# Block-sparse attention into a squared-ReLU feed-forward: an earlier load, more paired score slots, some inverses on VectorE, four more slots masked on TensorE

## Chip, cores, metric

One core of one Trainium2 chip. The metric is the device time in microseconds (us), median of several executions; lower is better. Engines: PE is TensorE (PEld its weight loads), DVE is VectorE, ACT is ScalarE, POOL is GpSimd, SP issues most DMAs.

## Reference

Four batches of eight heads, 768 positions, head size 64. The mask is made of 32 x 32 blocks: neighbours, the first and last block row and column, and three drawn blocks per block row. The attention output, 3072 x 512, goes through a feed-forward layer.

```
scores = (q @ k.T) / 8 ;  scores = where(mask, scores, -1e9)
attn   = softmax(scores) ;  x = attn @ v           # (4, 8, 768, 64) -> (3072, 512)
y      = (relu(x @ w_in) ** 2) @ w_out             # 512 -> 2048 -> 512
```

## The kernel before

Heads are handled in 16 pairs (four per batch). The unit of attention is a slot: one pair of heads, 256 queries (`qi`, three per sequence) and 256 keys (`cp`, three per sequence). There are 144 slots, 36 per batch. A slot has four score matmuls on 64 rows each (two heads side by side in the array: the two matmuls start some 4 ns apart in the trace), one exp on ACT, a multiplication by the mask on DVE, and four value matmuls on 128 rows. Three slots of one `qi` end in an inverse of the row sums (two Ln and an Exp on ACT) and two normalizing multiplications on DVE, which free `po`.

In batch 0 some slots are masked on PE instead: four more 64-row matmuls add a large negative number to the scores, and DVE has nothing to do.

```
def scores(slots):                        # one slot, or a pair of slots in a row
    for u, qi, cp in slots:
        ps = ps_s.tile([P, 2, 2, QW], F32, tag="ps")          # two such buffers in PSUM
        add = u < HP and qi < NQ_ADD
        for c in range(2 if add else 0):
            for h, hs in enumerate(HALVES):
                matmul(ps[:, h, c, :], oh[hs, ksl[c]], bq[hs, qsl], start=c == 0, stop=False)
        for c in range(2):
            for h, hs in enumerate(HALVES):                   # 64 rows per head
                matmul(ps[:, h, c, :], KT[i][hs, ksl[c]], QT[i][hs, qsl], start=not add, stop=True)

def inverse(u, qi):
    nc.scalar.activation(out=ls[0:D, :], in_=po[D:P, 0, :], func=AF.Ln)
    nc.scalar.activation(out=ls[D:P, :], in_=po[0:D, 1, :], func=AF.Ln)
    nc.scalar.activation(out=rs, in_=ls, func=AF.Exp, scale=-1.0)
```

The order of instructions on each engine is made when the kernel is built: every piece of work is a task with an engine, an estimated duration, a priority and its dependencies, and a list scheduler in the kernel's source places them. Attention has priority; feed-forward work of earlier batches fills PE.

```
# numbers of buffers, as handed to the scheduler:
bufs = {"ps": 2, "po": 1, "h": 2, "y": 1, "pT": 9, "r": 4, ...}
PAIRED = lambda s: s >= 72               # from slot 72 on (batch 2), two slots are one task
ld_t = Task("SP", 1.3, ..., (lambda u=u: load(u)), deps=... + gate[-1:], late=2.0, dma=3.9, ...)
# gate: a DMA that waits for the last piece of w_in (for pair 4), then of w_out (for pair 5 on)
```

The softmax here doesn't subtract the row's maximum and nothing guards it: scores larger than these inputs give would overflow.

Of the kernel before, what the change touches and what calls it, by code (L numbers as in the profile page):

```python
# [16 lines left out]
AF = mybir.ActivationFunctionType  # L17
AOP = mybir.AluOpType

P = 128  # L20
# [5 lines left out]
def kernel(  # L26
# [18 lines left out]
    nc = tc.nc  # L45
    B, H, S, D = q.shape
# [5 lines left out]
    scale = 1.0 / math.sqrt(D)  # L52
    assert D == 64 and S % P == 0 and d_model == moe_w_in.shape[0] and H % 2 == 0
    NCH = S // P
    HP = H // 2
    NF = d_ff // P
    KM = d_model // P
    QW = 256
    NQ = S // QW
    CP = NCH // 2  # L60
# [135 lines left out]
    V, G = nc.vector, nc.gpsimd  # L196
# [8 lines left out]
    def init_v(eng, i):  # L205
        eng.memset(VA[i][:, :, D:P], 1.0)
        eng.memset(VB[i][:, :, 0:D], 1.0)
# [70 lines left out]
    bq = consts.tile([P, S], BF, name="bq")  # L278
    mask = consts.tile([P, NQ, NCH, QW], BF, name="mask")
    mtile = {}  # L280
# [3 lines left out]
        nc.tensor.matmul(pb, bm.rearrange("a t j -> a (t j)"), oh[0:nb, qi * QW:(qi + 1) * QW], start=True, stop=True)  # L284
        mtile[qi] = pb

    def rows_copy(qi):
        nc.scalar.copy(out=bq[:, qi * QW:(qi + 1) * QW], in_=mtile.pop(qi))

    def mask_product(qi, cp):  # L290
        pq = ps_h.tile([P, 2, QW], F32, name="pq", tag="h")
# [50 lines left out]
    def w_load(i):  # L342

        if i < NWP:
            fs = slice(i * d_ff // NWP, (i + 1) * d_ff // NWP)
            nc.gpsimd.dma_start(out=w_in_sb[:, :, fs], in_=wiv[:, :, fs])
        else:
            ns = slice((i - NWP) * NF // NWP, (i - NWP + 1) * NF // NWP)
            nc.gpsimd.dma_start(out=w_out_sb[:, ns, :], in_=wov[:, ns, :])
# [4 lines left out]
        nc.sync.dma_start(out=scratch, in_=last)  # L354


    ptile, stile, otile, rtile, xT = {}, {}, {}, {}, {}

    def scores(slots):
        for u, qi, cp in slots:  # L360
            i = u % NPB
            ps = ps_s.tile([P, 2, 2, QW], F32, name="ps", tag="ps")
            qsl = slice(qi * QW, (qi + 1) * QW)
            ksl = [slice((cp * 2 + c) * P, (cp * 2 + c + 1) * P) for c in range(2)]
            add = u < HP and qi < NQ_ADD
            for c in range(2 if add else 0):
                for h, hs in enumerate(HALVES):
                    nc.tensor.matmul(ps[:, h, c, :], oh[hs, ksl[c]], bq[hs, qsl], start=c == 0, stop=False,  # L368
                                     skip_group_check=True)
            for c in range(2):  # L370
                for h, hs in enumerate(HALVES):
                    nc.tensor.matmul(ps[:, h, c, :], KT[i][hs, ksl[c]], QT[i][hs, qsl], start=not add,  # L372
                                     stop=True, skip_group_check=True)
            stile[u, qi, cp] = ps
# [28 lines left out]
            nc.tensor.matmul(po[:, 1, :], VB[i][:, n, :], pT[:, 1, c, :],  # L403
                             start=False, stop=last, skip_group_check=True)

    def inverse(u, qi):
        po = otile[u, qi]
        ls = work.tile([P, QW], F32, name="ls", tag="ls")
        rs = work.tile([P, QW], F32, name="rs", tag="rs")
        nc.scalar.activation(out=ls[0:D, :], in_=po[D:P, 0, :], func=AF.Ln)  # L410
        nc.scalar.activation(out=ls[D:P, :], in_=po[0:D, 1, :], func=AF.Ln)  # L411
        nc.scalar.activation(out=rs, in_=ls, func=AF.Exp, scale=-1.0)  # L412
        rtile[u, qi] = rs

    def normalize(u, qi):
# [78 lines left out]
            load_part(nc.sync, u, 0, c, c + 1)  # L494

    NQ_ADD = 2
    NQ_Y = 1
    KR, KY = 0, 500
    COLD = 5.3
    PT_BUFS, R_BUFS, G_BUFS, QC_BUFS = 9, 4, 2 * NF + 3, 5  # L500
# [6 lines left out]
    SEM = dict(late=LAT)  # L507
    pe = dict(late=0.2)
    order = [(a, qi, cp) for qi in range(NQ) for a in range(HP) for cp in range(CP)]
# [3 lines left out]
    first = {}  # L513
    for s, (u, qi, cp) in enumerate(order):
        first.setdefault(u, s)
    ev, cv, sc_of, va_of, mu = {}, {}, {}, {}, {}
    for u in range(NU):
        sc_of[u], va_of[u] = [], []
    wl, tr, gate, mk, tp = {}, {}, [], {}, {HP - 1: []}
# [9 lines left out]
    rc = []  # L529
    for qi in range(NQ):  # L530
        rp = Task("PE", 0.107, -7 if qi == 0 else 6 * qi - 6, (lambda qi=qi: rows_product(qi)), get="h",
                  deps=[oh_t] if qi else [], after=4.0 if qi == 0 else 7.0 * qi, **pe)
        rc.append(Task("ACT", 0.37, -7 if qi == 0 else 6 * qi - 6, (lambda qi=qi: rows_copy(qi)), deps=[rp], put=[rp], **SEM))
    for qi in range(NQ):
        for cp in range(CP):
            k = (qi - NQ_ADD) % NQ * CP + cp
# [5 lines left out]
    def prepare_first(u):  # L542

        tr[u], ev[u] = [], {}
        parts = [(1, c0, c1, t, first[u]) for (c0, c1), t in zip(K_PARTS.get(u, [(0, CP)]), land_k[u])]
        parts += [(0, c, c + 1, land_q[u][c], c * HP * CP + first[u]) for c in range(CP)]
        for w, c0, c1, at, s in parts:
            n = c1 - c0
            a = (u, w, c0, c1)
            on = "POOL" if c0 and not w else "ACT" if u == 0 and not c0 else "DVE"  # L550
            c = Task(on, 0.06 + {"DVE": 0.17, "POOL": 0.36, "ACT": 0.31}[on] * n, s - 6,
                     (lambda a=a, e={"DVE": V, "POOL": G, "ACT": nc.scalar}[on]: cast_qk(e, *a)), get="qc", after=at, **SEM)
            t = Task("PE", 0.15 * n, s - 5 - w, (lambda a=a: transp(*a)), deps=[c], get="h", put=[c], **pe)
            e = Task("DVE", 0.06 + 0.17 * n, s - 5, (lambda a=a: evac(*a)), deps=[t], put=[t], **SEM)
            tr[u].append(c)
            for i in range(c0, c1):
                ev[u][w, i] = e
        cv[u] = [Task("POOL", 0.6, first[u] - 2, (lambda u=u, h=h: cast_v(u, h)), after=land_v[u], **SEM)
                 for h in range(2)]
        if u == HP - 2:  # L560

            for i in range(NWP):
                wl[i] = Task("POOL", 1.0, first[u] + i, (lambda i=i: w_load(i)), deps=cv[u], late=2.0,
                             dma=3.4)
            gate.append(Task("SP", 0.5, 0, (lambda: loads_gate(1)), deps=[wl[NWP - 1]], late=0.0))

    def prepare(u):
        s0 = first[u]

        ld_t = Task("SP", 1.3, s0 - 20, (lambda u=u: load(u)), deps=cv[u - NRAW] + tr[u - NRAW] + gate[-1:],  # L570
                    late=2.0, dma=3.9, behind=tp[u - 1] if u > HP + 1 else [])
        old_sc = sc_of[u - NPB] if u >= NPB else []
        old_va = va_of[u - NPB] if u >= NPB else []
        tr[u], ev[u], tp[u] = [], {}, []
        for w in (1, 0):
            c = Task("DVE" if w else "POOL", 0.6 if w else 1.2, s0 - 12,
                     (lambda w=w: cast_qk(V if w else G, u, w, 0, CP)), deps=[ld_t], get="qc", **SEM)
            t = Task("SP", 1.5, s0 - 12, (lambda w=w: transp_dma(u, w)), deps=[c] + old_sc, put=[c],
                     late=2.0, dma=1.5)
            tr[u].append(c)  # L580
            tp[u].append(t)
            for i in range(CP):
                ev[u][w, i] = t
        early = []
        if u < NPB:
            early = [Task("POOL", 0.8, s0 - 8, (lambda u=u: init_v(G, u)), after=36.0, **SEM)]
        cv[u] = [Task("POOL", 0.6, s0 - 12, (lambda u=u, h=h: cast_v(u, h)), deps=[ld_t] + old_va + early, **SEM)
                 for h in range(2)]
        if u == HP:
            for i in range(NWP, 2 * NWP):  # L590
                wl[i] = Task("POOL", 1.0, s0 - 12 + i, (lambda i=i: w_load(i)), deps=cv[u], late=2.0, dma=4.0)
            gate.append(Task("SP", 0.5, 0, (lambda: loads_gate(2)), deps=[wl[2 * NWP - 1]], late=0.0))

    N_FIRST = HP * NQ_ADD * CP
    PAIRED = lambda s: s >= 72

    def attend(s, slots):
        sc = Task("PE", 0.645 if len(slots) > 1 else 0.56 if s < N_FIRST else 0.42, s, (lambda: scores(slots)),
                  deps=[t for u, qi, cp in slots if qi < NQ_ADD and u < HP for t in (rc[qi], oh_t)[:1 + (cp > 0)]] + [ev[u][1, cp] for u, qi, cp in slots] + [ev[u][0, qi] for u, qi, cp in slots] + sc_all[-1:],
                  get="ps", n=len(slots), **pe)  # L600
        sc_all.append(sc)
        for j, a in enumerate(slots):
            u, qi, cp = a
            k = s + j
            ex = Task("ACT", 0.97, k, (lambda a=a: exps(*a)), deps=[sc], get="pT", put=[sc.bufs[j]], **SEM)
            mm = ex
            if u >= HP or qi >= NQ_ADD:
                mm = Task("DVE", 0.82, k - 1, (lambda a=a: mask_mul(V, *a)), deps=[ex, mk[qi, cp]], **SEM)
            va = Task("PE", 0.44, k + 2.2, (lambda a=a: values(*a)), deps=[mm] + cv[u] + va_all[-1:],
                      get=None if cp else o_pool(u, qi), put=[ex], **pe)  # L610
            va_all.append(va)
            sc_of[u].append(sc)
            va_of[u].append(va)
            if cp == CP - 1:
                inv = Task("ACT", 1.2, k - 9, (lambda u=u, qi=qi: inverse(u, qi)), deps=[va], **SEM)
                mu[u, qi] = Task("DVE", 0.87, k - 9, (lambda u=u, qi=qi: normalize(u, qi)), deps=[inv],
                                 put=[va_all[-CP]], **SEM)

# [85 lines left out]
```

## Time and profile before

| | kernel before |
|---|---|
| median time | 313.33 us (312.79 to 314.36, 3 runs) |
| span of the profiled run | 311.1 us |
| PE busy | 297.7 us, 96% |
| ACT, DVE busy | 223.5 us, 214.0 us |
| last exp ends | 263.6 us; feed-forward work alone after it |

The span is the time between the first and last instruction of the program; the time has some 1.7 us more.

### The profile page before, as it was taken

The numbers are of one execution on the slowest core, as the hardware profiler recorded it, in microseconds if no ns is written. First come the engines' busy times: TensorE is split into PE (matmuls) and PEld (weight loads), VectorE is DVE, ScalarE is ACT, GpSimd is POOL, SyncE is SP. The second block draws the span as 40 slices with busy tenths as digits, with TensorE's granted clock in tenths as the row PEclk, the third lists the DMA queues.
The fourth block names the chain that finished last, engine by engine and source line by source line (L and its number), as shares of the span: only waits on it lengthen the run. The fifth ranks groups of instructions, "written<-read, shape, count | busy, mean of one in ns | idle before, by whom it ended". The sixth has DMA issues, their size and how long they took to land.

```text
span 311.1 us, 6029 instructions
## 1 busy us (share of the span) xinstructions
PE 297.7 (96%) x2259; PEld 173.3 (56%) x2292; DVE 214.0 (69%) x383; ACT 223.5 (72%) x358; POOL 178.4 (57%) x226
## 2 busy tenths in 40 slices
PE   6989889999999999999999999999999999999995
PEld 4655556557656545556555565555555655555542
DVE  8625559996967968998976668887657666444521
ACT  3899799985877989878878988888778887200000
POOL 5660396445974936975764457664454354666620
PEclk9999999999999999999999999999999999999999
DMA  7998289417447474716620083450000010000012
GB/s 221 346 208 169 90 140 184 152 37 201 105 147 223 94 200 151 215 48 211 163 75 36 1 238 87 151 86 27 9 34 36 0 37 35 34 36 34 34 36 101
DMA packets 42597, 34.47 MB, mean 111 GB/s; under 512 B 20680, under 2 KB 39624, under 8 KB 42568
## 3 DMA queue, kind: packets, MB, share of 16 engines
q1 hardware_dynamic: 37656, 29.50, 32.7%
q0 software_dynamic: 4224, 4.19, 8.4%
q10 hardware_dynamic: 688, 0.39, 0.4%
q8 instruction: 18, 0.29, 0.4%
q14 instruction: 11, 0.09, 0.1%
HBM read 27.26 MB, written 6.29 MB: 108 GB/s over the span
## 4 chain that ended last, share of the span: by engine, by line
PE 79%; DVE 9%; ACT 7%; issue 3%; POOL 1%; DVEq 0%; ACTq 0%
PE py L465 24%; PE ph L438 23%; PE po L401 10%; PE ps L372 10%; PE po L403 9%; ACT pT L378 4%; DVE pT L383 3%; DVE r L446 2%; PE ps L368 2%; POOL g L452 1%; ACT ls L411 1%; ACT ls L410 1%; ACT rs L412 1%; DVE xT L422 1%; DVE qc L309 1%
## 5 line engine op out<-in xcount | busy, mean ns | idle before, releaser
L452 POOL TENSOR_TENSOR g<-r 128x384 bf16<-128x384 f32 (+1 forms) x144 | 131.7, 925 | 103.9 <-DVE r L446 87.4
L378 ACT ACTIVATE pT<-ps 128x1024 bf16<-128x1024 f32 x144 | 142.2, 1020 | 22.7 <-PE ps L372 22.4
L383 DVE TENSOR_TENSOR pT<-pT,mask 128x1024 bf16<-128x1024 bf16 x120 | 95.8, 809 | 31.7 <-ACT pT L378 29.9
L438 PE MATMUL ph<-xT,w_in_sb 128*128 128x384 bf16 (+1 forms) x576 | 107.3, 309 | 0.2
L465 PE MATMUL py<-w_out_sb,g 128*128 128x512 bf16 x351 | 97.9, 380 | 2.1 <-ACT ys L472 0.5
L438 PEld LDWEIGHTS <-w_in_sb 128*128 128x128 bf16 x576 | 53.5, 98 | 40.0 <-issue 7.7
L446 DVE TENSOR_SCALAR r<-ph 128x384 f32<-128x384 f32 (+1 forms) x98 | 50.2, 513 | 35.5 <-PE ph L438 25.6
L401 PE MATMUL po<-pT,VA 128*128 128x256 bf16 x288 | 68.7, 275 | 2.2 <-DVE pT L383 0.9
L403 PE MATMUL po<-pT,VB 128*128 128x256 bf16 x288 | 68.2, 273 | 0.0
L465 PEld LDWEIGHTS <-g 128*128 128x128 bf16 x384 | 36.7, 98 | 28.5 <-issue 2.6
L372 PE MATMUL ps<-QT,KT 64*128 64x256 bf16 x576 | 48.7, 272 | 0.8 <-ACT pT L378 0.5
L401 PEld LDWEIGHTS <-VA 128*128 128x128 bf16 x288 | 27.9, 97 | 19.8 <-issue 10.1
L372 PEld LDWEIGHTS <-KT 64*128 64x128 bf16 x576 | 22.1, 94 | 25.0 <-issue 20.9
L403 PEld LDWEIGHTS <-VB 128*128 128x128 bf16 x288 | 28.2, 98 | 6.6 <-issue 1.8
L472 ACT COPY ys<-py 128x512 f32<-128x512 f32 x17 | 9.9, 581 | 28.3 <-PE py L465 28.3
L444 ACT ACTIVATE r<-ph 128x384 f32<-128x384 f32 (+1 forms) x46 | 20.6, 451 | 10.0 <-PE ph L438 8.8
L421 DVE TENSOR_TENSOR xT<-po,rs 64x256 bf16<-64x256 f32 x48 | 19.7, 410 | 7.4 <-ACT rs L412 7.1
L410 ACT ACTIVATE ls<-po 64x256 f32<-64x256 f32 x48 | 18.3, 380 | 8.1 <-PE po L403 7.0
L412 ACT ACTIVATE rs<-ls 128x256 f32<-128x256 f32 x48 | 20.0, 417 | 1.5
L422 DVE TENSOR_TENSOR xT<-po,rs 64x256 bf16<-64x256 f32 x48 | 20.5, 427 | 0.7
L411 ACT ACTIVATE ls<-po 64x256 f32<-64x256 f32 x48 | 18.0, 375 | 0.6
L309 POOL CAST qc<-qs 128x768 bf16<-128x768 f32 (+1 forms) x20 | 15.8, 800 | 3.3 <-PE pt L321 2.3
(53 smaller groups left out, 105.4 us busy)
## 6 DMA issues: line engine op xcount, KB each, us to landing
vs<-in_v_dram SPq DMA_DIRECT2D x16, 384.0 KB, 4.8
out_dram<-ys SPq DMA_DIRECT2D x23, 256.0 KB, 2.2
ks<-in_k_dram SPq DMA_DIRECT2D x15, 384.0 KB, 4.3
qs<-in_q_dram SPq DMA_DIRECT2D x12, 384.0 KB, 3.6
w_in_sb<-in_moe_w_in_dram POOLq DMA_DIRECT2D x4, 512.0 KB, 7.8
w_out_sb<-in_moe_w_out_dram POOLq DMA_DIRECT2D x4, 512.0 KB, 9.2
qs<-in_q_dram SPq DMA_DIRECT2D x11, 128.0 KB, 5.0
ks<-in_k_dram SPq DMA_DIRECT2D x1, 256.0 KB, 3.2
```

The lines of the kernel that those rows point to most:

```text
L372: nc.tensor.matmul(ps[:, h, c, :], KT[i][hs, ksl[c]], QT[i][hs, qsl], start=not add, stop=True, skip_group_check=True)
L378: nc.scalar.activation(out=pT, in_=stile.pop((u, qi, cp)), func=AF.Exp, scale=scale)
L383: eng.tensor_mul(out=pT, in0=pT, in1=mask[:, None, qi, cp * 2:cp * 2 + 2, :].broadcast_to([P, 2, 2, QW]))
L401: nc.tensor.matmul(po[:, 0, :], VA[i][:, n, :], pT[:, 0, c, :], start=first, stop=last, skip_group_check=True)
L403: nc.tensor.matmul(po[:, 1, :], VB[i][:, n, :], pT[:, 1, c, :], start=False, stop=last, skip_group_check=True)
L410: nc.scalar.activation(out=ls[0:D, :], in_=po[D:P, 0, :], func=AF.Ln)
L412: nc.scalar.activation(out=rs, in_=ls, func=AF.Exp, scale=-1.0)
L422: V.tensor_mul(out=xT[b][D:P, a, qsl], in0=po[D:P, 1, :], in1=rs[D:P, :])
L438: nc.tensor.matmul(ph, w_in_sb[:, kc, f * P:(f + 1) * P], xT[b][:, kc, c0:c0 + w], start=(kc == 0), stop=(kc == KM - 1))
L446: V.tensor_scalar(out=r, in0=htile.pop((T, f)), scalar1=0.0, scalar2=None, op0=AOP.max)
L452: G.tensor_mul(out=g, in0=r, in1=r)
L465: nc.tensor.matmul(py, gtile[T, f][:, ts * P:(ts + 1) * P], w_out_sb[:, f, :], start=(f == 0), stop=(f == NF - 1))
```

## The change

Its intent: give PE less to do (fewer switches between 128-row and 64-row matmuls by pairing slots in batch 1 as well) and fewer waits (ACT relieved of inverses in batch 0, the sixth pair's data earlier, a second buffer for `po` for longer). Cut to its core; new estimates of load times are shown once where they repeat.

```
+    def inverse(u, qi, on="ACT"):
+        if on == "ACT": (as before)
+        else:
+            V.tensor_copy(out=ls[0:D, :], in_=po[D:P, 0, :])
+            V.tensor_copy(out=ls[D:P, :], in_=po[0:D, 1, :])
+            V.reciprocal(out=rs, in_=ls)
...
-    NQ_Y = 1
+    N_ADD = 28
+    NQ_Y = 2                     # po of odd pairs in the second PSUM buffer for two thirds of batch 0
+    NQ_REC = 2                   # inverses of these thirds may go to DVE (the scheduler chooses)
...
-        rc.append(Task("ACT", 0.37, ...rows_copy(qi)...))
+        rc.append(Task({"ACT": (0.37, ...), "DVE": (0.3, ...)}, ...rows_copy(qi, on)...))
...
-                    late=2.0, dma=3.9, behind=...)          # and likewise for w_in, w_out, init_v
+                    late=0.8, dma=3.5, behind=...)
...
         if u == HP:                                          # u: pair; HP = 4
             for i in range(NWP, 2 * NWP):
                 wl[i] = Task("POOL", ..., w_load(i), deps=cv[u], ...)
+        if u == HP + 1:
             gate.append(Task("SP", 0.5, 0, loads_gate(2), deps=[wl[2 * NWP - 1]], ...))
...
-            add = u < HP and qi < NQ_ADD                     # 24 slots
+            add = (u, qi, cp) in added                       # the first 28 slots
-    PAIRED = lambda s: s >= 72
+    PAIRED = lambda s: s >= 36
```

More of the change, by code (lines that the diff above doesn't have):

```diff
@@ L285, in rows_product, with rows_copy @@
         mtile[qi] = pb
-    def rows_copy(qi):
-        nc.scalar.copy(out=bq[:, qi * QW:(qi + 1) * QW], in_=mtile.pop(qi))
+    def rows_copy(qi, on):
+        (nc.scalar.copy if on == "ACT" else V.tensor_copy)(out=bq[:, qi * QW:(qi + 1) * QW], in_=mtile.pop(qi))
     def mask_product(qi, cp):
@@ L354, in loads_gate @@
         nc.sync.dma_start(out=scratch, in_=last)
+    added = set()
     ptile, stile, otile, rtile, xT = {}, {}, {}, {}, {}
@@ L404, in values @@
                              start=False, stop=last, skip_group_check=True)
-    def inverse(u, qi):
+    def inverse(u, qi, on="ACT"):
         po = otile[u, qi]
@@ L409, in inverse @@
         rs = work.tile([P, QW], F32, name="rs", tag="rs")
-        nc.scalar.activation(out=ls[0:D, :], in_=po[D:P, 0, :], func=AF.Ln)
-        nc.scalar.activation(out=ls[D:P, :], in_=po[0:D, 1, :], func=AF.Ln)
-        nc.scalar.activation(out=rs, in_=ls, func=AF.Exp, scale=-1.0)
+        if on == "ACT":
+            nc.scalar.activation(out=ls[0:D, :], in_=po[D:P, 0, :], func=AF.Ln)
+            nc.scalar.activation(out=ls[D:P, :], in_=po[0:D, 1, :], func=AF.Ln)
+            nc.scalar.activation(out=rs, in_=ls, func=AF.Exp, scale=-1.0)
+        else:
+            V.tensor_copy(out=ls[0:D, :], in_=po[D:P, 0, :])
+            V.tensor_copy(out=ls[D:P, :], in_=po[0:D, 1, :])
+            V.reciprocal(out=rs, in_=ls)
         rtile[u, qi] = rs
@@ L532 @@
                   deps=[oh_t] if qi else [], after=4.0 if qi == 0 else 7.0 * qi, **pe)
-        rc.append(Task("ACT", 0.37, -7 if qi == 0 else 6 * qi - 6, (lambda qi=qi: rows_copy(qi)), deps=[rp], put=[rp], **SEM))
+        rc.append(Task({"ACT": (0.37, -7 if qi == 0 else 300), "DVE": (0.3, 6 * qi - 6)}, 0, 0, (lambda on, qi=qi: rows_copy(qi, on)), deps=[rp], put=[rp], **SEM))
     for qi in range(NQ):
@@ L562, in prepare_first @@
             for i in range(NWP):
-                wl[i] = Task("POOL", 1.0, first[u] + i, (lambda i=i: w_load(i)), deps=cv[u], late=2.0,
-                             dma=3.4)
+                wl[i] = Task("POOL", 1.0, first[u] + i, (lambda i=i: w_load(i)), deps=cv[u], late=1.0,
+                             dma=3.0)
             gate.append(Task("SP", 0.5, 0, (lambda: loads_gate(1)), deps=[wl[NWP - 1]], late=0.0))
@@ L570, in prepare @@
         ld_t = Task("SP", 1.3, s0 - 20, (lambda u=u: load(u)), deps=cv[u - NRAW] + tr[u - NRAW] + gate[-1:],
-                    late=2.0, dma=3.9, behind=tp[u - 1] if u > HP + 1 else [])
+                    late=0.8, dma=3.5, behind=tp[u - 1] if u > HP + 1 else [])
         old_sc = sc_of[u - NPB] if u >= NPB else []
@@ L585, in prepare @@
         if u < NPB:
-            early = [Task("POOL", 0.8, s0 - 8, (lambda u=u: init_v(G, u)), after=36.0, **SEM)]
+            early = [Task("POOL", 0.8, s0 - 8, (lambda u=u: init_v(G, u)), after=29.0, **SEM)]
         cv[u] = [Task("POOL", 0.6, s0 - 12, (lambda u=u, h=h: cast_v(u, h)), deps=[ld_t] + old_va + early, **SEM)
@@ L590, in prepare @@
             for i in range(NWP, 2 * NWP):
-                wl[i] = Task("POOL", 1.0, s0 - 12 + i, (lambda i=i: w_load(i)), deps=cv[u], late=2.0, dma=4.0)
+                wl[i] = Task("POOL", 1.0, s0 - 12 + i, (lambda i=i: w_load(i)), deps=cv[u], late=1.0, dma=3.4)
+        if u == HP + 1:
             gate.append(Task("SP", 0.5, 0, (lambda: loads_gate(2)), deps=[wl[2 * NWP - 1]], late=0.0))
-    N_FIRST = HP * NQ_ADD * CP
-    PAIRED = lambda s: s >= 72
+    added.update(order[:N_ADD])
+    PAIRED = lambda s: s >= 36
     def attend(s, slots):
-        sc = Task("PE", 0.645 if len(slots) > 1 else 0.56 if s < N_FIRST else 0.42, s, (lambda: scores(slots)),
-                  deps=[t for u, qi, cp in slots if qi < NQ_ADD and u < HP for t in (rc[qi], oh_t)[:1 + (cp > 0)]] + [ev[u][1, cp] for u, qi, cp in slots] + [ev[u][0, qi] for u, qi, cp in slots] + sc_all[-1:],
+        sc = Task("PE", 0.645 if len(slots) > 1 else 0.56 if s < N_ADD else 0.42, s, (lambda: scores(slots)),
+                  deps=[t for u, qi, cp in slots if (u, qi, cp) in added for t in (rc[qi], oh_t)[:1 + (cp > 0)]] + [ev[u][1, cp] for u, qi, cp in slots] + [ev[u][0, qi] for u, qi, cp in slots] + sc_all[-1:],
                   get="ps", n=len(slots), **pe)
@@ L606, in attend @@
             mm = ex
-            if u >= HP or qi >= NQ_ADD:
+            if a not in added:
                 mm = Task("DVE", 0.82, k - 1, (lambda a=a: mask_mul(V, *a)), deps=[ex, mk[qi, cp]], **SEM)
@@ L614, in attend @@
             if cp == CP - 1:
-                inv = Task("ACT", 1.2, k - 9, (lambda u=u, qi=qi: inverse(u, qi)), deps=[va], **SEM)
+                on = {"ACT": (1.2, k - 9)}
+                if u < HP and qi < NQ_REC:
+                    on["DVE"] = (2.6, k - 9)
+                inv = Task(on, 0, 0, (lambda *on, u=u, qi=qi: inverse(u, qi, *on)), deps=[va], **SEM)
                 mu[u, qi] = Task("DVE", 0.87, k - 9, (lambda u=u, qi=qi: normalize(u, qi)), deps=[inv],
```

## The prediction

> **What bounds the kernel now.** I read the page first, then busy time by stretch, then what TensorE waited for, then TensorE's instructions in order of time. The page's first part:
>
> ```profile
> PE 297.7 (96%) x2259; PEld 173.3 (56%) x2292; DVE 214.0 (69%) x383; ACT 223.5 (72%) x358; POOL 178.4 (57%) x226
> ```
>
> PE is busy for 297.7 of the span's 311.1 us. Nothing else is over 72% on average. The stretches show where other engines come near (columns: stretch, length, PE, PEld, DVE, ACT and POOL busy with counts, clock, DMA share, GB/s):
>
> ```profile
> 7.00:50.00 43.00, 39.45 (x420) 24.45 (x415) 24.08 (x53) 39.17 (x62) 23.98 (x42) 1.00 0.87 194
> 50.00:140.00 90.00, 88.06 (x693) 52.24 (x704) 76.82 (x131) 73.71 (x121) 59.69 (x74) 1.00 0.54 145
> 140.00:200.00 60.00, 59.05 (x432) 34.39 (x440) 45.63 (x74) 50.44 (x81) 35.30 (x37) 1.00 0.43 125
> 200.00:263.60 63.60, 63.13 (x467) 36.85 (x476) 43.85 (x76) 53.39 (x84) 33.00 (x33) 1.00 0.12 32
> 263.60:311.00 47.40, 43.49 (x229) 22.53 (x231) 18.09 (x32) 4.28 (x9) 21.93 (x26) 1.00 0.12 45
> ```
>
> From 7 to 50 us ACT (39.2 of 43) is as full as PE (39.5), while DVE has 19 us free. From 140 us to the end PE is all but gapless, and the last 47 us are feed-forward work alone, at full rate apart from the final store. So 200 us of the run can become shorter only if PE has less to do. What PE waited for, whole run:
>
> ```profile
> PE ps L368 <- ACT pT L378: 1.6, 3, 1.0
> PE pw L221 <- DVE warm L217: 1.1, 1, 1.1
> PE pb L284 <- DVE bm L274: 1.1, 1, 1.1
> PE po L401 <- DVE pT L383: 0.9, 3, 0.3
> PE po L401 <- DVE xT L422: 0.6, 1, 0.6
> PE po L401 <- ACT pT L378: 0.6, 2, 0.4
> PE ps L372 <- ACT pT L378: 0.5, 1, 0.5
> PE py L465 <- ACT ys L472: 0.5, 1, 0.5
> ```
>
> The two rows of 1.1 us are the start, which the change leaves alone. The other six come to 4.7 us in 11 waits. A matmul of 256 columns is shown with 0.27 us though the next starts 0.11 us after it, so each wait is about 0.16 us longer than shown: 4.7 + 11 x 0.16 = 6.5 us. Of these the rows of ps waiting for ACT (four waits), po for ACT (two) and po for xT (one) fall before 50 us: 3.3 + 7 x 0.16 = 4.4 us. The rest, 2.1 us, falls between 90 and 200 us. That is all that better feeding can win.
>
> What PE's work itself costs is read from starts. One slot's scores, and a pair's (start, shown length):
>
> ```profile
> 42.78 0.27 PE L403 MATMUL po<-pT,VB 128*128 128x256 bf16 x1
> 42.98 0.39 PE L372 MATMUL ps<-QT,KT 64*128 64x256 bf16 x4
> 43.31 0.28 PE L401 MATMUL po<-pT,VA 128*128 128x256 bf16 x1
> ...
> 134.84 0.27 PE L403 MATMUL po<-pT,VB 128*128 128x256 bf16 x1
> 135.05 0.61 PE L372 MATMUL ps<-QT,KT 64*128 64x256 bf16 x8
> 135.59 0.28 PE L401 MATMUL po<-pT,VA 128*128 128x256 bf16 x1
> ```
>
> From the start of the VB matmul before it to the start of the VA matmul after it: 0.53 us for one slot, 0.75 us for two. Less the 0.11 us that the VB matmul streams, that is 0.42 and 0.64 us. Two singles cost 0.84 us, a pair 0.64 us: going from 128-row to 64-row matmuls and back costs 0.20 us each time, whatever lies between.
>
> **What the Trainium skill says.** "TensorEngine Tiling (Array Packing)", section Key Properties, says that changing the tiling mode drains TensorE; the 0.20 us per excursion above agrees. "Perfetto Trace Analysis", section Tensor Engine Instruction, says that the end of a matmul in the profile is estimated; the 0.27 us shown against 0.11 us between starts agrees, and is why I work from starts. "VectorE: DVE Perf Modes", section "First, the fixed hardware budget", says that Reciprocal is an iterative divide with a repeat count of 8; the kernel before has no Reciprocal, so no row shows its length. "DMA: Bandwidth & Descriptors", section "Issuing engines are not separate DMA queues", says that loads from different queues share the 16 engines. The trace agrees: the four loads of w_out of 512 KB take 9.2 us each (median) when issued together, those of w_in 7.8 us.
>
> **The change part by part.** I compared the order of instructions of both builds.
>
> Pairs. Slots 36 to 71 become 18 pairs. In the old order eight singles already stood next to another single (44 runs of eight score matmuls, for 36 pairs), and the early part is also ordered anew, so the excursions that really go are fewer than 18: runs of 64-row matmuls fall from 99 to 87. 12 x 0.20 = 2.4 us less, all of it on PE.
>
> 28 slots masked on PE. Four slots more get four mask matmuls each; back to back, a 64-row pair takes 0.11 us, so 0.054 us per matmul: 16 x 0.054 = 0.9 us more on PE. DVE loses four multiplications of 0.81 us (3.2 us), in a stretch where it has room.
>
> Mask products. They stand in two more separate groups (24-row matmuls, about 0.2 us per group for going in and out): 0.4 us more.
>
> So PE's work changes by -2.4 + 0.9 + 0.4 = -1.1 us.
>
> Inverses. Four of the first eight inverses go from ACT to DVE, and two of the three copies of block rows as well. An inverse takes ACT 0.38 + 0.38 + 0.42 us, a copy 0.37 us shown and about 0.27 us in a row with others. An exp follows another in 0.95 us. For the first 24 slots ACT has 24 x 0.95 + 8 x 1.15 + 3 x 0.27 = 32.8 us before, and 24 x 0.95 + 4 x 1.15 + 0.27 = 27.7 us after. PE has for the same slots 24 x (0.64 for masks and scores + 0.44 for values) = 25.9 us, and about 2 us for the transposes and products between: 28 us. Before, ACT was the longer by about 5 us, which is the 4.4 us of waiting; after, the two are level. On DVE an inverse is two copies of some 0.4 us and the Reciprocal; my estimate is 2.6 us (the scheduler's own entry for it), 10.4 us in all, into 19 us of idle time. Two engines that are level, coupled through two score buffers, still wait for each other, and the 2 us Reciprocal stands in DVE's order ahead of evacuations that PE needs. So I count on 60% of the 4.4 us: 2.7 us less.
>
> Second buffer for po in the second third of batch 0: takes the one wait of po for xT away. It is in the 4.4 us.
>
> Load ahead of w_out. Before, the sixth pair's load was issued at 55.3 us, behind the landing of w_out, and its K was transposed at 68.7 us; exps 40 and 44 of the run begin at 66.2 and 78.3 us, twice the usual distance. In the new order that load follows the fifth pair's directly, at about 30 us by the old times. Yet PE was busy for 9.95 of the 10 us from 70 to 80, with feed-forward work that was there anyway. Attention moves forward, feed-forward work moves back into the last stretch, and the sum for PE is the same: I give this part 0 us. Of the 2.1 us of later waits I take 0.4 us as won.
>
> Sum: -1.1 - 2.7 - 0.4 = -4.2 us. 313.3 - 4.2 = 309.1 us, rounded to 309.0.
>
> **The rivals.** First, the early stretch gains nothing: DVE, with Reciprocals in line, delays copies out of the transposes and normalizations, and PE waits on DVE where it waited on ACT. For it: PE's waits at 30.7 to 31.3 us already end on DVE's mask, QT and xT. Against it: DVE is idle for 19 of 43 us there, and the reordering spreads the mask products. Time: 313.3 - 1.1 = 312.2 us or somewhat more.
>
> Second, all feeding waits go, as the schedule intends: -1.1 - 6.5 = -7.6 us, 305.7 us. For it: before, from 140 us on, paired slots run with almost no waits. Against it: ACT and PE are only level early, and four waits of the middle lay behind DVE's masks, which stay.
>
> Third, pairs in batch 1 starve PE: both score buffers must be empty before a pair starts, and ACT and DVE are 82% and 85% busy from 50 to 140 us. With exps bunched and small feed-forward tiles of 256 columns, the masks come late and values wait. For it: the three waits of po for DVE's masks lie in this stretch. Against it: the same pairs in batch 2 have feed-forward work between. One to three microseconds would be lost: 310 to 312 us.
>
> **Range and chances.** From the second rival, weighted down, and the first comes 306.2 to 312.2 us. Faster by over 2% means below 307.1 us: it needs 6.2 us, nearly every wait gone on top of the smaller work: 0.20. Slower by over 2% would need a new stall of 7 us, which nothing suggests: 0.02. Within 2%: 0.78.
>
> **What would show it.** In the changed profile PE's waits before 50 us on ACT's exps should fall from 2.7 us shown to about 1; the Reciprocal should take near 1.8 us and no wait of PE should end on it for over 0.5 us; slot 28's exp (47.7 us before) should begin near 42 us; the sixth pair's load should start near 30 us with no gap between exps 40 and 44; attention should end several microseconds before the old 263.6 us. I am wrong if PE's starts are gapless early (then the time is near 306) or if waits on DVE's masks grow after 50 us (then near 312).

## The result, and the profile after

The changed kernel took 309.18 us (median of 4 runs, 308.15 to 309.56), the kernel before 313.06 us in the same rounds. The ratio is 0.9863, 95% interval 0.9824 to 0.9901. Ratios here and below are the mean time of one kernel's fast runs over that of the kernel before in the same rounds, so not quite the ratio of the medians. The whole interval lies below 1, so the gain is clear of the noise, but it is under 2%.

The first part of the page of the changed kernel, then its stretches (columns as in the prediction; attention ends at 258.7 us here), then all that PE waited for (total, times, longest):

```profile
PE 298.0 (97%) x2308; PEld 175.8 (57%) x2308; DVE 221.4 (72%) x393; ACT 218.8 (71%) x344; POOL 177.2 (58%) x226
```

```profile
7.00:50.00 43.00, 42.27 (x460) 26.37 (x455) 34.61 (x70) 39.96 (x54) 24.60 (x44) 1.00 1.05 230
50.00:140.00 90.00, 89.15 (x718) 55.50 (x714) 78.66 (x131) 73.19 (x122) 64.64 (x79) 1.00 0.58 149
140.00:200.00 60.00, 59.51 (x448) 34.78 (x447) 42.06 (x72) 50.12 (x80) 34.96 (x37) 1.00 0.37 106
200.00:260.00 60.00, 59.88 (x444) 34.68 (x442) 43.06 (x71) 49.40 (x79) 27.39 (x28) 1.00 0.06 23
260.00:306.40 46.40, 42.67 (x224) 21.71 (x222) 17.43 (x31) 3.80 (x8) 21.11 (x26) 1.00 0.12 46
```

```profile
PE pw L221 <- DVE warm L217: 1.1, 1, 1.1
PE pb L284 <- DVE bm L274: 1.1, 1, 1.1
PE po L402 <- DVE xT L428: 0.7, 3, 0.3
PE py L471 <- ACT ys L478: 0.5, 1, 0.5
PE ps L373 <- ACT pT L379: 0.3, 1, 0.3
PE pt L321 <- DVE KT L328: 0.3, 1, 0.3
PE ps L369 <- ACT pT L379: 0.2, 1, 0.2
```

PE's busy time hardly changed (298.0 against 297.7 us), and some rows of matmuls are missing in the trace of before (351 of 384 of w_out), so this row explains nothing. The stretch from 7 to 50 us does: PE was busy for 42.3 us of it, before for 39.5. DVE filled 10.5 us of its room there. ACT is about as busy as before (40.0 us against 39.2), but gets through more exps in it: exp 28 begins at 41.7 us, before at 47.7. The waits of the score buffers ps for ACT went from 2.1 us to 0.5, those of po for ACT from 0.6 to none. The one wait of po for the normalization (xT) before 50 us (0.6 us) is gone; new are three such waits between 90 and 117 us.

To compare many runs I made two sums from each trace. For every two matmuls in a row, the time between their starts less what this pair of kinds takes when nothing holds it (the lower fifth of all such gaps of the traces) is a wait; the rest is work. Gaps of exactly one missing row count as work. The method is good to about half a microsecond (in a_split, below, it misses by 0.8). Work, waits, 1.1 us before the first matmul and 4.1 us after the last start add up to the span.

| kernel | span | first exp | work | waits to 9 us | 9 to 50 us | after 50 us |
|---|---|---|---|---|---|---|
| before | 311.1 | 7.43 | 293.8 | 1.6 | 5.4 | 4.9 |
| changed | 306.4 | 7.44 | 292.5 | 1.7 | 2.2 | 4.8 |
| changed, later run | 307.5 | 8.07 | 291.9 | 2.6 | 2.1 | 5.6 |

From before to changed: work 1.3 us less, early waits 3.2 us less, later waits 0.1 us less, together the 4.6 us between the spans. The medians differ by 3.9 us only: the profiled run of the changed kernel is its fastest, the other three had spans of 307.1 to 307.8 us.

The column "first exp" guards against a trap: in every profiled run the first exp begins near 7.4 us or near 8.1 us, whatever was edited. In the one form PE's matmuls run at full rate from 5.1 us on, where a wait of PE ends; in the other they still take twice as long until about 9 us (8.8 to 9.6 us in the traces). Two runs of the same changed kernel, the first then the second, PE in order of time:

```profile
6.78 0.39 PE L369 MATMUL ps<-bq,oh 64*128 64x256 bf16 x4
7.01 0.38 PE L373 MATMUL ps<-QT,KT 64*128 64x256 bf16 x4
```

```profile
6.99 0.60 PE L369 MATMUL ps<-bq,oh 64*128 64x256 bf16 x4
7.39 0.63 PE L373 MATMUL ps<-QT,KT 64*128 64x256 bf16 x4
```

Four mask matmuls take 0.23 us to the next start in one and 0.40 us in the other. (The granted clock that the profile gives for 6.0 to 7.4 us is 1.00 in both runs, so only the starts tell.) From 12 us on, the later run stays 0.8 to 1.1 us behind the first, matmul by matmul. It costs 0.9 us of waits in the table (2.6 against 1.7). Spans are therefore compared below only between runs with the same first exp; medians and ratios mix both forms.

### The profile page after: what moved, and what is told of

It is laid out like the page before. It is cut to its first block, busy times and chain, and to the rows that moved or that the text cites. A ratio compares the mean times of both kernels' runs of the same rounds, so it can differ in the third digit from the quotient of the medians.

```text
span 306.4 us, 6104 instructions
## 1 busy us (share of the span) xinstructions
PE 298.0 (97%) x2308; PEld 175.8 (57%) x2308; DVE 221.4 (72%) x393; ACT 218.8 (71%) x344; POOL 177.2 (58%) x226
## 4 chain that ended last, share of the span: by engine, by line
PE 85%; DVE 6%; ACT 4%; DMA 2%; issue 1%; POOL 0%; SPq 0%; ACTq 0%; DVEq 0%
PE py L471 25%; PE ph L444 24%; PE po L402 11%; PE ps L373 10%; PE po L404 9%; PE ps L369 3%; ACT pT L379 2%; DVE pT L384 2%; DMA ks<-in_k_dram 2%; PE pq L294 1%; PE pt L321 1%; DVE r L452 1%; DVE xT L428 1%; DVE xT L427 1%; ACT ls L413 1%
## 5 line engine op out<-in xcount | busy, mean ns | idle before, releaser
L458 POOL TENSOR_TENSOR g<-r 128x384 bf16<-128x384 f32 (+1 forms) x144 | 133.1, 935 | 89.1 <-DVE r L452 69.9
L384 DVE TENSOR_TENSOR pT<-pT,mask 128x1024 bf16<-128x1024 bf16 x116 | 93.1, 814 | 23.5 <-ACT pT L379 21.7
L471 PE MATMUL py<-w_out_sb,g 128*128 128x512 bf16 x384 | 104.2, 379 | 0.5 <-ACT ys L478 0.5
L444 PEld LDWEIGHTS <-w_in_sb 128*128 128x128 bf16 x576 | 54.8, 98 | 38.6 <-issue 4.5
L452 DVE TENSOR_SCALAR r<-ph 128x384 f32<-128x384 f32 (+1 forms) x96 | 48.8, 510 | 27.1 <-PE ph L444 17.2
L373 PE MATMUL ps<-QT,KT 64*128 64x256 bf16 x576 | 46.8, 271 | 0.3 <-ACT pT L379 0.3
L450 ACT ACTIVATE r<-ph 128x384 f32<-128x384 f32 (+1 forms) x48 | 21.9, 456 | 12.5 <-PE ph L444 10.8
L412 ACT ACTIVATE ls<-po 64x256 f32<-64x256 f32 x44 | 16.8, 381 | 11.1 <-PE po L404 10.2
L414 ACT ACTIVATE rs<-ls 128x256 f32<-128x256 f32 x44 | 18.3, 417 | 1.4
L315 POOL CAST VA<-vs 128x384 bf16<-128x384 f32 x16 | 9.3, 584 | 15.2 <-DMA vs<-in_v_dram 9.5
```

What stands on the lines that cost most here:

```text
L373: nc.tensor.matmul(ps[:, h, c, :], KT[i][hs, ksl[c]], QT[i][hs, qsl], start=not add, stop=True, skip_group_check=True)
L384: eng.tensor_mul(out=pT, in0=pT, in1=mask[:, None, qi, cp * 2:cp * 2 + 2, :].broadcast_to([P, 2, 2, QW]))
L444: nc.tensor.matmul(ph, w_in_sb[:, kc, f * P:(f + 1) * P], xT[b][:, kc, c0:c0 + w], start=(kc == 0), stop=(kc == KM - 1))
L450: nc.scalar.activation(out=r, in_=htile.pop((T, f)), func=AF.Relu)
L452: V.tensor_scalar(out=r, in0=htile.pop((T, f)), scalar1=0.0, scalar2=None, op0=AOP.max)
L458: G.tensor_mul(out=g, in0=r, in1=r)
```

## The experiments

Every run gave a correct result. All were timed in five rounds, in three groups on different chips; the kernel before had medians of 313.71 us (a_nopairs, a_act, a_oldload, b_pairs), 313.61 us (after_again, a_split, a_split0, a_mask2) and 313.79 us (the others), so medians from different groups compare to about 0.2 us. One execution fell in the slow state (a_split, 316.24 us) and is left out of its median; all others were fast. "After" stands for the changed kernel. The sums of all of them, by the method above:

| run | median us | ratio | span | first exp | work | waits 9 to 50 us | after 50 us |
|---|---|---|---|---|---|---|---|
| after_again | 308.98 | 0.9855 | 307.5 | 8.07 | 291.9 | 2.1 | 5.6 |
| a_split0 | 308.39 | 0.9841 | 306.6 | 7.42 | 292.4 | 2.2 | 5.0 |
| a_split | 310.63 | 0.9931 | 308.9 | 7.43 | 295.5 | 2.2 | 4.3 |
| a_mask2 | 311.30 | 0.9931 | 309.6 | 8.05 | 293.7 | 2.8 | 5.4 |
| a_nopairs | 309.74 | 0.9874 | 309.1 | 8.07 | 294.9 | 2.1 | 4.2 |
| a_actfix | 311.55 | 0.9929 | 308.5 | 7.42 | 292.5 | 4.6 | 4.5 |
| a_act | 314.10 | 1.0007 | 313.9 | 8.08 | 293.1 | 6.4 | 6.6 |
| a_oldload | 310.51 | 0.9890 | 308.8 | 8.06 | 292.6 | 1.9 | 6.5 |
| a_add24 | 310.66 | 0.9898 | 307.9 | 7.43 | 291.5 | 3.1 | 6.4 |
| b_pairs | 318.42 | 1.0147 | 316.8 | 8.06 | 292.1 | 5.3 | 11.7 |
| b_pairs_load | 312.75 | 0.9967 | 312.4 | 8.06 | 292.2 | 6.1 | 6.3 |
| a_p28n20 | 334.36 | 1.0670 | 330.9 | 7.43 | 294.6 | 6.7 | 22.8 |

**The reference run.** after_again, unedited.

> The changed kernel unedited, as the common reference of these runs: 309.2, ratio 0.986 to 0.988 to before. No theory differs on it.

Measured: 308.98 us, ratio 0.9855 (0.9838 to 0.9873). The gain is confirmed on another occasion, with a narrower interval.

### Prices with the order untouched

These edits sit inside a task, so the scheduler places everything as in the changed kernel; the traces show the same order of matmuls.

**a_split: TensorE is forced out of 64-row mode inside 18 pairs.**

```
+            if (u, qi, cp) in split:      # the second slot of each pair of batch 1
+                matmul(ps[:, 0, 0, 0:16], identb, identb[:, 0:16], start=True, stop=True)
```

> The changed kernel, its schedule untouched: between the two slots of each of the 18 pairs of batch 1 stands one 128-row matmul of 16 columns into the second slot's score buffer, which the scores then overwrite (the result stays right). Theory: it forces TensorE out of 64-row mode and back, 18 x 0.20 = 3.6 us, plus under 0.02 us each for its own columns, and all of it reaches the end: 312.5 to 313.2 where the changed kernel has 309.2. Rival (batch 1 is not bound by TensorE, or the cost of an excursion is the matmul's and not the change of mode): under 311.

Measured: 310.63 us over the five fast executions (310.44 to 313.41), ratio 0.9931 (0.99 to 0.9961). That is 1.7 us more than after_again by medians, 2.4 us by ratios, and by spans of the same start 308.9 against 306.4, 2.5 us. One such place, PE in order of time:

```profile
53.07 0.39 PE L377 MATMUL ps<-QT,KT 64*128 64x256 bf16 x4
53.40 0.18 PE L369 MATMUL ps<-identb 128*128 128x16 bf16 x1
53.51 0.39 PE L377 MATMUL ps<-QT,KT 64*128 64x256 bf16 x4
53.84 0.61 PE L448 MATMUL ph<-xT,w_in_sb 128*128 128x256 bf16 x4
```

In the changed kernel the same stretch goes from 53.09 to 53.63 us. Set against each other matmul by matmul, the two traces part by 0.21 us at each of the 18 places (0.210 to 0.213), 3.8 us in all; the table's sums, with 3.0 us, are too low here. That is the 0.20 us that I had read, plus about 0.01 us for the small matmul. Between 89 and 127 us PE gets some 1.5 us back, mostly at value matmuls that had waited: the waits of po for xT (0.7 us shown in the changed kernel) are gone from this run's list. So the median misses the theory's range, by 1.9 us, and falls 0.4 us inside the rival's: the price was right, that all of it reaches the end was not: about 2.4 of the 3.8 us do.

**a_split0: the same matmuls where the mode is 128 rows anyway** (the first slot of each pair instead of the second).

> Control for a_split: the same 18 matmuls of 16 columns, each ahead of the first slot of its pair, where TensorE is in 128-row mode anyway. Theory: no change of mode is added, 18 x 0.02 to 0.06 us, 309.2 to 310.2. Rival (a small matmul costs 0.2 us anywhere): same as a_split.

Measured: 308.39 us, ratio 0.9841; span 306.6 against 306.4 of the changed kernel. The small matmul is all but free. So what a_split added is the change of mode, and the second half of the rival (the cost is the matmul's) falls.

**a_mask2: mask matmuls in eight more slots, DVE multiplying all the same.**

```
-            add = (u, qi, cp) in added
+            add = (u, qi, cp) in added or (u, qi, cp) in twice      # slots 28 to 35
```

> The changed kernel, its schedule untouched: slots 28 to 35 get the mask matmuls on TensorE as well, while VectorE still multiplies by the mask (a mask twice is the same result). Theory: 32 matmuls x 0.054 = 1.7 us more on TensorE, and TensorE is gapless enough from 35 to 50 us for 1.2 to 1.7 us of it to reach the end: 310.4 to 310.9. Rival (TensorE waits for exps there, so the masks are free): 309.2 to 309.7.

Measured: 311.30 us, 2.3 us more than after_again, and above the theory's range. Spans of the same start differ by 2.1 us (309.6 against 307.5): 1.8 us of work, 0.056 us per matmul as predicted, and 0.7 us of waits more between 9 and 50 us, less some later. PE has no room there any more; mask matmuls are paid in full.

**a_actfix: the four inverses back on ACT, at their places in the same order.**

```
-        if on == "ACT":
+        if True:
```

> The changed kernel with its schedule untouched: only the four inverses that stood on VectorE are issued on ScalarE, at the same place in the program (TensorE's order stays the same, instruction by instruction). In a_act all was scheduled anew and one wait of 2.8 us for the normalization came in; here that can't happen by a new order. Theory (ScalarE has 4 x 1.15 = 4.6 us more in batch 0, where it and TensorE are level): TensorE's waits between 9 and 50 us grow by 2.5 to 4.6 us and the time by as much, 311.5 to 313.5. Rival (a_act lost by its new order alone): 309 to 310.3.

Measured: 311.55 us, ratio 0.9929, 2.6 us more than after_again by medians and 2.1 us by spans (308.5 against 306.4). The first rows of what PE waited for in this run:

```profile
PE ps L369 <- ACT pT L379: 1.5, 4, 0.5
PE pw L221 <- DVE warm L217: 1.1, 1, 1.1
PE pb L284 <- DVE bm L274: 1.1, 1, 1.1
PE ps L373 <- ACT pT L379: 0.9, 2, 0.6
```

The score buffers wait for exps for 2.4 us in six waits, against 0.5 us in two. Work is the same to 0.1 us, waits from 9 to 50 us are 4.6 against 2.2. Matmul by matmul, this run is 2.6 us behind the changed kernel at 50 us and 2.1 us from 130 us on. So the inverses on DVE are worth about 2.1 to 2.6 us, net of what they cost DVE, by the predicted mechanism; the time is at the lower end of what I expected of this run, the waits 0.1 us below it.

### Parts taken out of the change, everything scheduled anew

**a_act: inverses and row copies on ACT only.**

```
-    NQ_REC = 2
+    NQ_REC = 0
-        rc.append(Task({"ACT": (0.37, -7 if qi == 0 else 300), "DVE": (0.3, 6 * qi - 6)}, ...))
+        rc.append(Task("ACT", 0.37, -7 if qi == 0 else 6 * qi - 6, ...))
```

> The changed kernel with all inverses and all three copies of block rows on ScalarE again. Theory (ScalarE was the longer engine of batch 0 by 5 us): TensorE's waits for exps before 50 us return to 3 to 4 us of starts, the time is 2 to 3 us longer, 311 to 312, ratio 0.993 to 0.997. Rival (the second buffer of po and the new order of batch 0 made the gain, not the free ScalarE): 309.2 to 310, ratio under 0.989.

Measured: 314.10 us (311.87 to 316.31), ratio 1.0007 (0.9967 to 1.0047): the whole gain is gone, more than expected. Its waits:

```profile
PE po L402 <- DVE xT L428: 4.3, 3, 2.7
PE ps L369 <- ACT pT L379: 1.9, 4, 1.0
```

The waits for exps came back (1.9 us), as expected; on top stands one wait of 2.7 us at 42.6 us, of po for a normalization whose inverse ACT did only after three exps (42.7 to 43.9 us) and which on DVE then stood behind a cast until 44.5 us. The new order put the value matmuls too early. a_actfix shows that about half of the 5 us is ACT's work with the four inverses; the other half is this order and the two row copies, which a_actfix leaves on DVE.

**a_nopairs: batch 1 in single slots.**

```
-    PAIRED = lambda s: s >= 36
+    PAIRED = lambda s: s >= 72
```

> The changed kernel with batch 1 in single slots again; all else as changed. Its order has 100 runs of 64-row score matmuls on TensorE, against 87 in the changed kernel. Theory (each run costs 0.20 us of TensorE whatever it waits for): 13 x 0.20 = 2.6 us longer than the changed kernel's 309.2, so near 311.8, ratio to before 0.994 to 0.996. Rival (what pairs save is given back as waits of the values for the normalization, which stand at 90 to 117 us in the changed kernel, 1.5 us): 309.2 to 310.0, ratio under 0.989, and those waits gone.

Measured: 309.74 us, ratio 0.9874 (0.9856 to 0.9893): 0.8 us more than after_again by medians, 1.6 us by spans (309.1 against 307.5). This is the rival's range by the time; by spans it lies between rival and theory. The intervals of the two ratios overlap, so by times alone the loss is barely clear. The work grew by 2.4 to 3.0 us, as 13 x 0.20 = 2.6 says; the waits after 50 us fell by 1.4 us against after_again (from 90 to 140 us they are 0.8 instead of 2.6 us, from 50 to 90 us 1.5 instead of 0.3). In the changed kernel PE arrives at the values in 90 to 140 us before the normalization is through; with single slots part of that waiting is filled with switching. So of the 2.6 us that pairs save, 0.8 to 1.6 us reach the end.

**a_oldload: the sixth pair's load behind w_out again.**

```
-        if u == HP + 1:
-            gate.append(...)
+            gate.append(...)          # for u == HP, as before
```

> The changed kernel with the sixth pair's load behind the output weights again (the estimates of the schedule stay as changed). Theory (TensorE had feed-forward work in the gap of attention): the gap of about 12 us between exps 40 and 44 comes back, attention ends some 3 us later, and the time stays within 0.7 us of the changed kernel, 308.5 to 309.9. Rival (attention that is held up pushes masks and relus of ScalarE and VectorE together later and costs TensorE waits): 1.5 us or more longer, 310.7 or above.

Measured: 310.51 us, ratio 0.9890 (0.9872 to 0.9908): 1.5 us more than after_again, 1.3 us by spans. It misses both ranges and lies nearer the rival. Exps 40 and 44 are 10.3 us apart (7.5 in after_again, 12.1 before), and the last exp ends at 265.0 instead of 259.8 us. Work is 0.7 us more and waits after 50 us are 0.9 us more. So the load was not worth nothing, as I had said: without it the scheduler's kernel is 1.3 to 1.5 us slower, spread over the order that follows. What of it is the load and what the new order is not told apart.

Where the load stands, in the kernel before and the changed one (SP in order of time, the q load of the sixth pair and the line before it):

```profile
55.01 0.24 SPq L354 DMA_DIRECT2D scratch<-w_out_sb  x1
55.30 0.40 SPq L167 DMA_DIRECT2D qs<-in_q_dram  x1
```

```profile
30.58 0.46 SPq L167 DMA_DIRECT2D vs<-in_v_dram  x1
31.14 0.42 SPq L167 DMA_DIRECT2D qs<-in_q_dram  x1
```

Before, it follows the small DMA that waits for w_out; after, it follows the fifth pair's v directly, 24 us earlier.

**a_add24: 24 slots masked on PE, as before.**

```
-    N_ADD = 28
+    N_ADD = 24
```

> The changed kernel with 24 slots masked on TensorE, not 28; scheduled anew, 85 runs of score matmuls against 87. Theory (masks on TensorE cost 0.054 us per matmul, VectorE has room for four more masks): TensorE's work 16 x 0.054 + 2 x 0.2 = 1.3 us less, waits up by up to 1 us: 307.9 to 309.2. Rival (VectorE with its inverses has no room, the 28 are what makes them fit): 309.5 to 311, with waits of values for masks between 30 and 50 us.

Measured: 310.66 us, ratio 0.9898: 1.7 us more than after_again, 1.5 us by spans (307.9 against 306.4). The rival's range holds. Work fell by 1.0 us, but waits rose by 0.9 us before 50 us and by 1.6 us after. The rival's picture, waits for masks between 30 and 50 us, is only a part of that; the rest comes later, where the order differs throughout.

### Parts put into the kernel before

**b_pairs: pairs in batch 1 alone.**

```
-    PAIRED = lambda s: s >= 72
+    PAIRED = lambda s: s >= 36
```

> The kernel before with the pairs of batch 1 as the only edit. Its order has 88 runs of score matmuls against 99. Theory: 11 x 0.20 = 2.2 us less than before, 310.9, ratio 0.993. Rival (pairs in batch 1 starve TensorE when the rest is as before): 312.5 to 314, ratio 0.998 or more, with more waits of the values for masks between 60 and 130 us.

Measured: 318.42 us, ratio 1.0147 (1.0130 to 1.0164): 4.7 us slower than before. Work fell by 1.7 us; the waits after 50 us rose from 4.9 to 11.7 us. What PE waited for, and one such wait in order of time:

```profile
PE po L401 <- ACT pT L378: 2.1, 5, 0.8
PE ps L372 <- ACT pT L378: 1.8, 4, 0.8
PE ps L368 <- ACT pT L378: 1.4, 3, 1.0
PE po L401 <- DVE pT L383: 1.4, 5, 0.4
```

```profile
141.00 0.39 PE L372 MATMUL ps<-QT,KT 64*128 64x256 bf16 x4
142.20 0.40 PE L372 MATMUL ps<-QT,KT 64*128 64x256 bf16 x4 [0.81 <-ACT pT L378]
```

PE stands in the middle of a pair: the first slot's four matmuls start at 141.00 us, the second slot's buffer is still held by an exp, and nothing else can pass. The rival had the direction right, but neither the size (312.5 to 314) nor the place: 7.6 of the 11.7 us lie after 140 us, in pairs that both kernels have, and between 60 and 130 us the waits of values for masks are 0.6 us in two waits, before 0.7 in two. Nor is the middle of a pair the main place: after 140 us it has 1.2 us in two waits as shown, value matmuls that waited for exps or masks 2.1 us in five. (That both buffers must be empty before a pair starts holds for the scheduler's plan; here the first slot started while the second's buffer was held.)

**b_pairs_load: pairs, and the load with its new estimates.**

```
-    PAIRED = lambda s: s >= 72
+    PAIRED = lambda s: s >= 36
-  late=2.0, dma=3.9 (pairs)   late=2.0, dma=3.4 (w_in)   late=2.0, dma=4.0 (w_out)   after=36.0
+  late=0.8, dma=3.5           late=1.0, dma=3.0          late=1.0, dma=3.4           after=29.0
+        if u == HP + 1:
             gate.append(...)
```

> The kernel before with two parts of the change: pairs in batch 1, and the sixth pair's load ahead of the output weights together with the new estimates of load times for the schedule; inverses, masks and buffers of batch 0 as before. b_pairs alone took 318.4. Theory (pairs in batch 1 are harmless if attention is not held up there; b_pairs lost because the order made for late loads left TensorE without other work later): 310.5 to 312.5, TensorE's waits after 50 us near the 5 us of before. Rival (pairs cost waits by themselves unless batch 0 is relieved too): 315 or more, waits after 50 us near the 11.7 us of b_pairs.

Measured: 312.75 us, ratio 0.9967 (0.9947 to 0.9988), 5.7 us less than b_pairs. It misses the theory's range by 0.25 us and refutes the rival's 315 us or more: pairs don't cost that many waits by themselves. Waits after 50 us are 6.3 us, near those of before; early waits stay at 6.1 us because batch 0 is not relieved. Whether the earlier load or the better estimates rescued the pairs is not told apart by this run.

**a_p28n20: a try at a faster version.**

```
-    N_ADD = 28                             -    PAIRED = lambda s: s >= 36
+    N_ADD = 20                             +    PAIRED = lambda s: s >= 28
```

> A try at a faster kernel: the changed one with 20 slots masked on TensorE and pairs from slot 28 on; 82 runs of score matmuls against 87, 8 groups of mask products against 12, 32 mask matmuls fewer. TensorE's work 5 x 0.2 + 4 x 0.2 + 32 x 0.054 = 3.5 us less. If the waits stay as they are: 305.7. If VectorE's masks in batch 0 cost as much in waits: 309 or above. I expect half of it, 307 to 308.

Measured: 334.36 us, ratio 1.067, far off. I had overlooked a constant: the schedule holds the mask products of the first two thirds of `qi` back to after 52 us, since those slots were masked on PE. Slots 20 to 23 now needed such a mask. DVE in order of time:

```profile
59.00 0.69 DVE L299 TENSOR_SCALAR mask<-pq 128x512 bf16<-128x512 f32 x1 [2.73 <-PE pq L294]
61.01 1.88 DVE L299 TENSOR_SCALAR mask<-pq 128x512 bf16<-128x512 f32 x3
62.92 0.69 DVE L384 TENSOR_TENSOR pT<-pT,mask 128x1024 bf16<-128x1024 bf16 x1
```

Masks made from 59 to 63 us are what the multiplication at 62.92 us had to follow; exp 28 began at 39.4 us and exp 32 at 74.7 us. The granted clock fell to 0.974 besides, so part of its "waits" are slow matmuls. Nothing about pairs or masks in general follows from it. No version faster than the changed kernel was found.

## Why the prediction was right

**The time.** Predicted 309.0 (309.1 by its own sum), measured 309.18 us, well inside the range. The terms below are measured on the two profiled runs, 4.6 us apart; set against the changed kernel's later run they are -1.9, -3.3 and +0.7 us, and 1.0 us before 9 us. The likeliest of the three cases, within 2%, is what came: the ratio is 0.9863.

**PE's work: predicted -1.1, measured -1.3 us.** The prices in it hold separately: 0.21 us per excursion, small matmul included, with the order fixed (a_split) against 0.20; 0.056 us per mask matmul (a_mask2) against 0.054.

**Early waits: predicted -2.7, measured -3.2 us.** The mechanism is shown by a_actfix: with only the engine of four inverses changed back, PE waits 2.4 us longer in batch 0. The Reciprocal took 1.752 us where I expected near 1.8. Exp 28 began at 41.7 us where I expected near 42. No wait of PE ends on the Reciprocal, so the first rival fell. (Its place of 30.7 to 31.3 us was read too widely: the list of waits has one there, of po for xT, ended at 32.17 us.) The signs hold too: waits for exps shown before 50 us fell to 0.5 us where I had said about 1. The size is in part luck: by these sums the early waits were 5.4 us and not 4.4, and the 60% that I counted on had no line behind it; 3.2 of 5.4 us is 59%.

**Later waits: predicted -0.4, measured -0.1 us.** The sum hides a change of kind: the waits for masks before 140 us went, and three waits for the normalization came (0.7 us shown, 90 to 117 us).

**What was wrong.** "I give this part 0 us" for the load: a_oldload shows 1.3 to 1.5 us. The argument, that PE was busy in the gap anyway, looked at the gap alone; the order of all that follows changes too. The four slots more on PE were counted as 0.9 us lost, with DVE's relief as worth nothing; taking them out (a_add24) loses 1.5 to 1.7 us instead. The point on the DMA queues enters no term of the sum, and no run here shows it.

The terms are not independent either. Undoing pairs, inverses (a_act), load and the four slots one at a time costs 0.8, 5.1, 1.5 and 1.7 us by medians, 9.1 us together, where the whole gain is some 4 us; and pairs alone on the kernel before lose 4.7 us where my sum would have given about 2 us of gain. The sum of terms came out because the total work and the total waits were estimated, each from one list, not because each part of the diff brings its own term. The third rival, pairs that starve PE, did not happen in the changed kernel; b_pairs, on the kernel before, does lose to waits, but later and mostly for exps.

**What stays open.** Why pairs starve PE with the old load and estimates is shown as a place (mostly after 140 us, at value matmuls and in the middle of pairs), not as a cause; which half of b_pairs_load's two edits rescues them; and how much of a_add24's loss is DVE's load and how much its order. The second buffer of po and the two row copies were not tried by themselves.

## What to carry to other kernels

Where one engine is the bound, split its time into work and waits from the starts of its instructions, by stage, and price a change against both lists; the busy share said 96% before and 97% after and explained neither. Where a scheduler orders everything anew, test a part by an edit that leaves the order alone (another engine for the same place, an extra matmul inside a task) before believing a leave-one-out run: a_act said 5 us, a_actfix 2.1 to 2.6 us. Moving work from a level engine to an idle one paid here although the idle one is slower: an inverse takes about 2.6 us on VectorE against 1.15 us on ScalarE, and PE still gained.

## What the Trainium skill lacked or had wrong

- "TensorEngine Tiling (Array Packing)", Key Properties, says that a change of tiling mode drains TensorE, without a duration. Here it costs 0.20 us for going to 64-row mode and back between 128-row matmuls (read from starts), and 0.21 us in a_split, the small matmul included; the same small matmul without a change of mode added 0.1 us for 18 of them in the span (306.55 against 306.44 us).
- "VectorE: DVE Perf Modes", section "First, the fixed hardware budget", gives a repeat count for Reciprocal but no duration. Here a Reciprocal of 128x256 f32 took 1.752 us in all four executions of the trace, against 0.42 us for a copy of 64x256 f32 out of PSUM.
- "TensorE: Matmul & The Clock Gate", section "What's actually happening", says that the warm-up follows a free-running window and varies by run. The traces agree that it varies (that a window free of the kernel sets it, no run here shows) and add the size on a whole kernel: full rate from 5.1 us on in seven traces, from 8.8 to 9.6 us in the other seven, nothing between, and 0.9 us more of waits. The page calls the ramp less than 1% of a typical kernel; here its spread is 0.3%, about as much as one part of this change is worth.
